# An attention and mixture-of-experts kernel: the attention steps written out as two rows of parts, and smaller routing tables

## The chip, the cores and the metric

The kernel runs on one core of one Trainium2 chip. The metric is the device time of one execution in microseconds (us). A core has five engines that each run their own list of instructions in order and wait for one another by semaphores: TensorE (PE; its weight loads are PEld), VectorE (DVE), ScalarE (ACT), GpSimd (POOL) and SyncE (SP). DMA transfers are issued from the lists of SP, ACT and POOL.

## What is computed

Attention with a linear bias and a window of 128 keys for 8 batches, 8 heads, 576 positions, 64 wide; then, for all 4608 rows, a dense two-layer network plus one of 8 experts, picked by the largest gate logit and weighted by its probability.

```python
scores = scale * q @ k.T;  rel = pos[:, None] - pos[None, :]
scores = where((rel >= 0) & (rel < 128), scores - slope * abs(rel), -1e9)
attn = exp(scores - max);  x = (attn / sum) @ v          # rows of 512: 8 heads x 64
y_dense = maximum(x @ w1_dense, 0) @ w2_dense
e = argmax(x @ w_gate);  gate = softmax(x @ w_gate)[e]
out = y_dense + gate * (maximum(x @ w1[e], 0) @ w2[e])
```

## The kernel before

**Attention.** The work comes in 16 units `u` (a batch and half of its heads, 4 heads), and a unit in three parts `pr`: query tiles 0 and 1, tiles 2 and 3, and the last 64 rows; 48 steps in all. A unit loads q and k (576 KB each, into `qraw` and `kraw`, one buffer each) and v; DVE transposes q and k (`turn`, L157), ACT rounds them (`round_qk`, L166), DVE makes the low half of v (`prep_v`, L176).

A step has this chain: PE writes the bias into `sq` (L371) and adds the scores (L383); ACT takes the exponential (L394, two halves); DVE subtracts the rounded part (`plo`, L413, two halves); PE multiplies by v into `ax` (`attend`, L447); DVE divides (`norm`, L462 and L463) into `xf`, of which there are two buffers; POOL copies `xf` into the row that is sent away (L469), PE transposes it (`flip`, L490) and ACT copies it twice (L497).

**Gate and dense part.** When a batch's six steps are done: logits (L511, L532), choice of expert (L543 to L554), counts on PE (L566, L574), slots (L584 to L601); POOL scatters the rows to `xs_dram` (L609, five transfers), and PE and ACT compute the dense network in 13 pieces (`dense1` L655 with ACT L662, `dense2` L670 with ACT L681), whose results POOL scatters to `ys_dram` (L682, five transfers). All of these pieces pass through two PSUM buffers (`psum_m`). POOL also loads the 18 expert and dense weight blocks (L89).

**Order.** The order on PE, ACT, DVE and SP is as the program issues it; on POOL a scheduler sets it. One loop over 49 passes issues in pass n: the transposes of step n-3, bias and scores and exponentials of step n, the norm of step n-2, `attend` of step n-1, then dense pieces and `turn`, `round_qk` or `prep_v` of the next unit, and last the `plo` of step n:

```python
if 0 <= n - 3 < NS: flip(*steps[n - 3])
if n < NS: lo = scores(u, pr)
if n - 2 in norms: norms.pop(n - 2)()
if 0 <= n - 1 < NS: norms[n - 1] = attend(*steps[n - 1])
... # dense pieces; turn, round_qk, prep_v of unit u + 1
if lo: lo()
```

**Experts.** After 6 batches a table (`route_early`) on one partition gives 16 blocks of 128 rows of one expert; after all 8 a second table (`late_table`) gives 27 more. For each of 43 blocks SP fetches the rows (`fetch`, L871), PE transposes them (L886), DVE brings the expert's first weights (`bring`, L907), PE does both layers (L918, L934), DVE adds (L942) and POOL scatters the result (L950). The leftovers of the last two batches stand between the first blocks.

Of the kernel before, what the change touches and what calls it, by code (L numbers as in the profile page):

```python
# [9 lines left out]
F32 = mybir.dt.float32  # L10
# [13 lines left out]
def kernel(  # L24
# [37 lines left out]
    NL = NB - NE  # L62

# [19 lines left out]
    def load_weights(i):  # L83
        e, wi = divmod(i, 2)
        if e == 0:
            e, src = E, (moe_w1_dense, moe_w2_dense)[wi]
        else:
            e, src = e - 1, (moe_w1, moe_w2)[wi][e - 1]
        nc.gpsimd.dma_start(  # L89
            out=w_all[:, e, wi, :, :],  # L90
            in_=src.rearrange("(ks p) f -> p ks f", p=P),
        )

# [19 lines left out]
    )  # L113

# [102 lines left out]
    last = (NU - 1) % NV  # L217
    order = [i for i in range(NV) if i != last]
    vfs = {i: abuf.tile([P, NT, 4, D + 1], F32, name=f"vf{i}") for i in order}
    for i in range(2):  # L220
        kT = abuf.tile([P, 2, SP_], F32R, name=f"kT{i}")
        nc.gpsimd.memset(kT.bitcast(F32)[:, :, S:SP_], 0.0)
        kTs.append(kT)
    vfs[last] = abuf.tile([P, NT, 4, D + 1], F32, name=f"vf{last}")
    for i in range(NV):
        nc.gpsimd.memset(vfs[i][TAIL:P, NT - 1, :, :], 0.0)
        nc.gpsimd.memset(vfs[i][:, :, :, D : D + 1], 1.0)
    for i in range(2):
        xrow = dbuf.tile([P, NT, RW], F32, name=f"xrow{i}")
        nc.gpsimd.memset(xrow[:, :, TC + 1 : RW], 0.0)  # L230
        xrows.append(xrow)
    lt = dbuf.tile([P, SP_ - DT[1][0] * P], F32, name="ltsb")
    nc.gpsimd.memset(lt, 0.0)
# [33 lines left out]
    def more_constants():  # L267
# [26 lines left out]
        nc.vector.tensor_copy(out=jf, in_=jf_i)  # L294
# [12 lines left out]
    jf = consts.tile([P, NB], F32, name="jf")  # L307
# [5 lines left out]
    def pool_constants():  # L313
# [15 lines left out]
        nc.gpsimd.iota(jf_i, pattern=[[1, NB]], base=0, channel_multiplier=0)  # L329
# [10 lines left out]
    jf_i = ints[:, 128 : 128 + NB]  # L340
    pool_constants()

# [7 lines left out]
    def scores(u, pr):  # L350
        hq = u % HQ
        qT = qkT[("q", u)]
        kT = qkT[("k", u)]
        kjs = KP[pr]
# [3 lines left out]
        wid = PW if len(kjs) == 2 else TAIL  # L358
        tot = wid * len(kjs)

        for rot, g in [(i, j) for i in range(4) for j in range(4)]:
# [16 lines left out]
            )  # L378
        for i, kj in enumerate(kjs):
# [11 lines left out]
        ps = []  # L391
        for i in range(2):
            p32 = ppool.tile([P, 2, tot], F32, name="p32", tag=f"p32_{tot}", bufs=4 if len(kjs) == 2 else 2)
            nc.scalar.activation(  # L394
                out=p32[:, :, 0:tot],
                in_=sq[i][:, :, 0:tot],
                func=ACT.Exp,
                scale=SCALE,
            )
            phi = p32.bitcast(BF16).rearrange("p g (c t) -> p g c t", t=2)[:, :, :, 1]  # L400
            plo = ppool.tile([P, 2, tot], BF16, name="plo", tag=f"plo_{tot}", bufs=4 if len(kjs) == 2 else 2)
            ps.append((p32, phi, plo))
        for i, kj in enumerate(kjs):
            for g in range(4):
                _, phi, plo = ps[g // 2]
                pbuf[(u, kj, g)] = (
                    phi[:, g % 2, i * wid : (i + 1) * wid],
                    plo[:, g % 2, i * wid : (i + 1) * wid],
                )

        def lo():
            for p32, phi, plo in ps:
                nc.vector.tensor_tensor(  # L413
                    out=plo[:, :, 0:tot],
                    in0=p32[:, :, 0:tot],
                    in1=phi[:, :, 0:tot],
                    op=ALU.subtract,
                )

        return lo  # L420
# [3 lines left out]
    def attend(u, pr):  # L424
# [29 lines left out]
        ax_v = ax[:, :, 0 : 4 * (D + 1)].rearrange("p t (h d) -> p t h d", h=4)  # L454

        def norm():
            if hq == 0 and pr == 0:
                cur[("xrow", b)] = xrows[b % 2]
            xrow = cur[("xrow", b)].bitcast(BF16)
            xf = xpool.tile([P, 2, 256], F32, name="xf", tag="xf")  # L460
            recip = gs.tile([P, 2, 4], F32, name="recip", tag="recip")
            nc.vector.reciprocal(out=recip[:rows, 0:nt], in_=ax_v[:rows, 0:nt, :, D])  # L462
            nc.vector.tensor_tensor(  # L463
                out=xf[:rows, 0:nt].rearrange("p t (h d) -> p t h d", h=4),
                in0=ax_v[:rows, 0:nt, :, 0:D],
                in1=recip[:rows, 0:nt].unsqueeze(3).to_broadcast([rows, nt, 4, D]),
                op=ALU.mult,
            )
            nc.gpsimd.tensor_copy(  # L469
                out=xrow[:rows, qis[0] : qis[0] + nt, hq * 256 : hq * 256 + 256],  # L470
                in_=xf[:rows, 0:nt],
            )
            cur[("xf", u, pr)] = cur["xf"] = xf

        return norm

    def flip(u, pr):
# [4 lines left out]
        if hq == 0 and pr == 0:  # L482
            cur[("xTb", b)] = xpool.tile([P, 4, S], BF16, name="xTb", tag="xTb")
        if pr == 0:
            cur["xT"] = xpool.tile([P, 2, S], F32, name="xT", tag="xT", bufs=1)
        xf = cur.pop(("xf", u, pr))
        tp = psum_m.tile([P, 2, 2, P], F32, name="tp", tag="misc")
        for i in range(nt):
# [7 lines left out]
        for dst in (cur["xT"], cur[("xTb", b)][:, 2 * hq : 2 * hq + 2, :]):  # L496
            nc.scalar.copy(  # L497
                out=dst[:, :, q0 : q0 + nt * rows].rearrange(
                    "p c (t x) -> p t c x", t=nt
                ),  # L500
                in_=tp[:, 0:nt, :, 0:rows],
            )
# [3 lines left out]
    def gate_a(u):  # L506
        lp = psum_m.tile([P, 512], F32, name="lp", tag="misc")
        for h, (t0, t1) in enumerate(DT):
            for c in range(2):
# [4 lines left out]
                    rhs=cur["xT"][:, c, t0 * P : t0 * P + LW],  # L514
# [3 lines left out]
        gst["lp"] = lp  # L518

    def gate_av(u):  # L520
        src, dst = gst["lp"][:, 0:LW], lt[:, 0:LW]
# [40 lines left out]
    def gate_c(b):  # L562
# [13 lines left out]
        )  # L576
        ex = gs.tile([P, NT, E], F32, name="ex", tag="ex")
        nc.scalar.activation(out=ex, in_=gst["lgs"], func=ACT.Exp)
        gst["ex"], gst["pc"] = ex, pc
# [12 lines left out]
    def gate_d(b):  # L592
        oh, ex, sl = ohs[b % 2], gst["ex"], gst["sl"]
        xrow = cur[("xrow", b)]
# [7 lines left out]
        nc.gpsimd.tensor_scalar_add(  # L602
# [4 lines left out]
        for t in range(NT):  # L607
            rows = min(P, S - t * P)
            ins = nc.gpsimd.indirect_dma_start(  # L609
                out=xs_dram[:, :],  # L610
                out_offset=bass.IndirectOffsetOnAxis(ap=slot[:rows, t : t + 1], axis=0),
                in_=xrow.bitcast(I32)[:rows, t, :],
                in_offset=None,
            )
            apart("x", b, ins)
        slots[b] = slot

# [26 lines left out]
    def dense1(b, c, hf):  # L644
        c0, c1 = DT[hf][0] * P, min(DT[hf][1] * P, S)
        HF = c1 - c0
        xTb = cur[("xTb", b)]
        if c == 0:
            cur["hT"] = xpool.tile(
# [505 lines left out]
```

## Time and profile before

| | before |
|---|---|
| median of 3 runs (lowest to highest) | 418.57 us (418.14 to 421.89) |
| the profiled execution's own time | 417.28 us |
| its span, first to last instruction | 415.6 us |
| last attention norm ends | 286.8 us |
| busy share of the span PE, DVE, ACT, POOL | 80%, 67%, 66%, 49% |

Shares over the whole span mix the attention stage (up to 287 us) with the expert stage (from there on); the rows below go by stage.

### The profile page before, as it was taken

The numbers are of one execution on the slowest core, as the hardware profiler recorded it, in microseconds if no ns is written. First come the engines' busy times: TensorE is split into PE (matmuls) and PEld (weight loads), VectorE is DVE, ScalarE is ACT, GpSimd is POOL, SyncE is SP. The second block draws the span as 40 slices with busy tenths as digits, with TensorE's granted clock in tenths as the row PEclk, the third lists the DMA queues.
The fourth block names the chain that finished last, engine by engine and source line by source line (L and its number), as shares of the span: only waits on it lengthen the run. The fifth ranks groups of instructions, "written<-read, shape, count | busy, mean of one in ns | idle before, by whom it ended". The sixth has DMA issues, their size and how long they took to land.

```text
span 415.6 us, 12698 instructions
## 1 busy us (share of the span) xinstructions
PE 333.6 (80%) x5003; PEld 228.2 (55%) x5003; DVE 280.3 (67%) x517; ACT 272.7 (66%) x430; POOL 202.0 (49%) x244
## 2 busy tenths in 40 slices
PE   3678887897788789789778976866975889999990
PEld 0455664564455456466555744544743557777770
DVE  5989897966769478686666879553433536666661
ACT  5859777977878597787669785734424445565550
POOL 4023317646444644863643586343173356555562
PEclk9999699999999899999969998997995999999996
DMA  7948799679967595997948816365866849999830
GB/s 204 263 103 166 178 213 216 178 195 217 242 143 182 170 213 169 211 213 184 229 161 171 218 61 125 100 200 165 271 200 216 318 137 311 331 293 334 274 144 14
DMA packets 76731, 82.43 MB, mean 198 GB/s; under 512 B 43519, under 2 KB 61311, under 8 KB 76672
## 3 DMA queue, kind: packets, MB, share of 16 engines
q1 hardware_dynamic: 58704, 47.32, 40.9%
q0 software_dynamic: 17680, 33.12, 30.9%
q10 hardware_dynamic: 288, 1.18, 0.8%
q8 instruction: 40, 0.66, 0.7%
q14 instruction: 19, 0.16, 0.1%
HBM read 64.20 MB, written 28.66 MB: 223 GB/s over the span
## 4 chain that ended last, share of the span: by engine, by line
PE 37%; DVE 19%; issue 12%; POOL 11%; ACT 9%; DMA 7%; another core or an unknown queue 2%; POOLq 1%; DVEq 0%; ACTq 0%; SPq 0%
DVE plo L413 9%; POOL out_dram L950 9%; PE ax L447 9%; PE yp L670 7%; PE hp L655 5%; ACT qT L166 4%; PE sq L383 3%; PE tp L490 3%; DVE xf L463 3%; PE hpm L918 2%; PE lg L532 2%; POOL xs_dram L609 2%; ACT p L394 2%; DVE qs L157 2%; DMA qraw<-in_q_dram 2%
## 5 line engine op out<-in xcount | busy, mean ns | idle before, releaser
L413 DVE TENSOR_TENSOR plo<-p 128x1024 bf16<-128x1024 f32 (+1 forms) x96 | 86.2, 938 | 40.7 <-ACT p L394 38.3
L394 ACT ACTIVATE p<-sq 128x1024 f32<-128x1024 f32 (+1 forms) x96 | 69.8, 784 | 21.2 <-PE ax L447 11.3
L447 PE MATMUL ax<-vf,p 128*128 128x65 bf16 (+1 forms) x576 | 66.7, 204 | 16.2 <-DVE xf L463 14.8
L447 PEld LDWEIGHTS <-p 128*128 128x128 bf16 (+1 forms) x1152 | 62.7, 106 | 30.7 <-DVE xf L463 20.3
L950 POOL DMA_INDIRECT out_dram<-yo,xr x43 | 49.0, 1138 | 52.5 <-DVE yo L942 36.3
L469 POOL CAST xrow<-xf 128x512 bf16<-128x512 f32 (+1 forms) x48 | 39.0, 813 | 69.2 <-DVE xf L463 66.2
L447 PE MATMUL ax<-vl,p 128*128 128x64 bf16 (+1 forms) x576 | 66.2, 200 | 0.7 <-issue 0.7
L447 PE MATMUL ax<-vf,plo 128*128 128x65 bf16 (+1 forms) x576 | 66.0, 201 | 0.9 <-issue 0.9
L942 DVE SCALAR_TENSOR_TENSOR yo<-y,xr,yr 128x512 f32<-128x512 f32 x43 | 32.3, 751 | 47.2 <-issue 17.6
L682 POOL DMA_INDIRECT ys_dram<-yt,slot x35 | 39.9, 1141 | 40.3 <-ACT yt L681 35.0
L447 PEld LDWEIGHTS <-plo 128*128 128x128 bf16 (+1 forms) x576 | 58.4, 105 | 1.1 <-issue 1.1
L655 PE MATMUL hp<-xTb,w_all 128*128 128x256 bf16 (+1 forms) x256 | 44.0, 302 | 7.7 <-ACT hTd L662 3.1
L609 POOL DMA_INDIRECT xs_dram<-xrow,slot x40 | 41.9, 1046 | 12.0 <-issue 10.4
L934 PE MATMUL y<-w_all,hTm 128*128 x172 | 45.8, 389 | 2.3 <-issue 1.2
L918 PE MATMUL hpm<-xTm,ws 128*128 128x128 bf16 x688 | 46.3, 221 | 1.6 <-ACT xTm L892 1.5
L383 PE MATMUL sq<-qT,kT 32*128 32x256 f32 (+2 forms) x640 | 32.5, 313 | 17.9 <-ACT qT L166 10.0
L670 PE MATMUL yp<-w_all,hTd 128*128 128x512 bf16 (+1 forms) x160 | 42.1, 389 | 3.7 <-DVE ltsb L523 1.9
L918 PEld LDWEIGHTS <-ws 128*128 128x128 bf16 x688 | 41.3, 99 | 3.1 <-issue 1.7
L662 ACT ACTIVATE hTd<-hp 128x256 bf16<-128x256 f32 (+1 forms) x64 | 25.8, 422 | 26.1 <-PE hp L655 18.1
L926 ACT ACTIVATE hTm<-hpm 128x512 bf16<-128x512 f32 x43 | 25.7, 598 | 23.0 <-PE hpm L918 11.9
L383 PEld LDWEIGHTS sq<-qT,kT 32*128 32x128 f32 x640 | 24.3, 199 | 27.7 <-ACT qT L166 12.6
L166 ACT CAST kT<-ks 128x1152 fp32r<-128x1152 f32 x16 | 37.8, 2360 | 1.8 <-DVE ks L157 1.8
(138 smaller groups left out, 553.0 us busy)
## 6 DMA issues: line engine op xcount, KB each, us to landing
yr<-ys_dram SPq DMA_DIRECT2D x43, 256.0 KB
kraw<-in_k_dram SPq DMA_DIRECT2D x16, 576.0 KB
vf<-in_v_dram SPq DMA_DIRECT2D x64, 128.0 KB
w_all<-in_moe_w_dram POOLq DMA_DIRECT2D x16, 512.0 KB
qraw<-in_q_dram SPq DMA_DIRECT2D x14, 576.0 KB
xr<-xs_dram SPq DMA_DIRECT2D x43, 130.0 KB
ys_dram<-fill_x SPq DMA_DIRECT2D x8, 256.0 KB
qraw<-in_q_dram ACTq DMA_DIRECT2D x2, 576.0 KB
```

The source lines that it names most:

```text
L166: copy(out=d[:, :, 0:S].rearrange("p c (x r) -> p c r x", r=R), in_=s.rearrange("p c (r x) -> p c r x", r=R),)
L383: nc.tensor.matmul(out=sq[g // 2][:, g % 2, i * wid : i * wid + nq], lhsT=kT[32 * g : 32 * g + 32, c, kj * P : kj * P + P], rhs=qT[32 * g ...
L394: nc.scalar.activation(out=p32[:, :, 0:tot], in_=sq[i][:, :, 0:tot], func=ACT.Exp, scale=SCALE,)
L413: nc.vector.tensor_tensor(out=plo[:, :, 0:tot], in0=p32[:, :, 0:tot], in1=phi[:, :, 0:tot], op=ALU.subtract,)
L447: nc.tensor.matmul(out=ax[:rows, i, o0 : o0 + w], lhsT=lhs, rhs=rhs, start=(n == 1), stop=(n == 3 * len(kl)),)
L609: ins = nc.gpsimd.indirect_dma_start(out=xs_dram[:, :], out_offset=bass.IndirectOffsetOnAxis(ap=slot[:rows, t : t + 1], axis=0), in_=xrow. ...
L655: nc.tensor.matmul(out=hp[:, 0:HF], lhsT=w_all[:, E, 0, kc, c * P : c * P + P], rhs=xTb[:, kc, c0:c1], start=(kc == 0), stop=(kc == 3),)
L670: nc.tensor.matmul(out=yp[:rows, :], lhsT=hT[:, c, t0 * P : t0 * P + rows], rhs=w_all[:, E, 1, c, :], start=(c == 0), stop=(c == 3),)
L682: ins = nc.gpsimd.indirect_dma_start(out=ys_dram[:, :], out_offset=bass.IndirectOffsetOnAxis(ap=slots[b][:rows, t : t + 1], axis=0), in_=y ...
L918: nc.tensor.matmul(out=hp[:, c, :], lhsT=ws[:, kc, c * P : (c + 1) * P], rhs=xT[:, kc, :], start=(kc == 0), stop=(kc == 3),)
L934: nc.tensor.matmul(out=y, lhsT=hT[:, c, :], rhs=w_all[:, bass.DynSlice(er, 1), 1, c, :], start=(c == 0), stop=(c == 3),)
L950: ins = nc.gpsimd.indirect_dma_start(out=out[:, :], out_offset=bass.IndirectOffsetOnAxis(ap=xr.bitcast(I32)[:, TC : TC + 1], axis=0), in_= ...
```

## The change

**Order.** `scores`, `flip` and the others are cut into parts, one for each piece on one engine, and named by a key: `mask` (the bias), `qk`, `exp`, `lo` (one half of `plo`), `ax`, `norm`, `xrow` (POOL's copy), `tp` (transpose), `xT` and `xTb` (ACT's two copies), `tk`, `tq`, `rk`, `rq`, `vl`, `lk`, `lq`, `lv` (loads), `lp`, `lt`, `lg`, `gb`, `pc`, `ex`, `cv`, `gd` (gate), `xs`, `ys` (POOL's scatters), `hp`, `hTd`, `yp`, `yt` (dense), `w` and `wd` (weights). The row `FIRST` (128 parts) orders batch 0. The row `CYCLE` (136 parts) is repeated for batches 1 to 7; a part marked `@1` or `@2` belongs to the batch one or two repetitions back, `@-1` to the next one. The numbers behind a name are half of the heads and step (or piece). POOL's parts of the attention stage are chained in this order too (`in_turn`). Two weight blocks go with each batch (four with batch 0); before, 18 over 42 steps.

**Routing tables.** They stand on 32 partitions, one block on each; the running sums over experts are one product with a triangle and one reduction (`sums`) in place of a copy and seven additions.

**Constants.** `more_constants` is issued before the first `turn`, and its POOL part before the memsets of `vf`, `kT` and `xrow`.

```diff
-        for n in range(NS + 1):
-            if 0 <= n - 3 < NS:
-                flip(*steps[n - 3])
...
+    CYCLE = """
+        xs:1@2 vl:0@0 tp:1,1@1 xTb:1,1@1 tq:1@0 xrow:1,0@1 xT:1,1@1
+        exp:0,0,1@0 lk:1@0 xs:3@2 ax:1,2@1 w:1@1 yp:0@2 yt:0@2 yp:1@2
...
+    for i, word in enumerate(CYCLE):
+        word, late = word.split("@")
+        for b in range(1, B):
+            put(b, word, ((b + int(late)) * L + i, 1, 0))
+    plan = sorted(left, key=left.get)
...
+        for key in plan:
+            at = left[key]
+            if at > end:
+                break
+            n = 6 * at[0] / L
+            do(*key)
...
+    def in_turn(ins):
+        if chain:
+            tc.add_manual_dep(
+                ins.ins,
+                chain[0],
...
+    def sums(cnt, nm):
+        m = rt.tile([RB, E, E], F32, name="m" + nm, tag="m")
+        nc.vector.tensor_tensor(
+            out=m, in0=tri, in1=cnt.unsqueeze(1).to_broadcast([RB, E, E]), op=ALU.mult
+        )
+        cb = small("cb" + nm)
+        nc.vector.tensor_reduce(out=cb, in_=m, op=ALU.add, axis=AX.X)
+        return cb
...
         mask_consts()
+        more_constants()
         turn(0, "k")
```

POOL, from one batch's row scatters on, before (`xs_dram` rows are `xs`, `ys_dram` rows `ys`; the number in a name is a buffer's):

```order
L609 DMA xs_dram<-xrow_144,slot 37888x260 x5
L469 CAST xrow_142<-xf 128x2x256
L701 CAST w_all<-xf 64x1
L89 DMA w_all<-in_moe_w_dram 128x4x512
L602 TENSOR_SCALAR xrow_144<-tok_c 128x5
L682 DMA ys_dram<-yt,slot 37888x512 x2
L469 CAST xrow_142<-xf 64x256
```

And now:

```order
L662 DMA xs_dram<-xrow_168,slot 37888x260
L510 CAST xrow_170<-xf 128x2x256
L662 DMA xs_dram<-xrow_168,slot 37888x260
L768 CAST w_all<-xf 64x1
L91 DMA w_all<-in_moe_w_dram 128x4x512
L510 CAST xrow_170<-xf 128x2x256
L662 DMA xs_dram<-xrow_168,slot 37888x260
L753 DMA ys_dram<-yt,slot 37888x512
L662 DMA xs_dram<-xrow_168,slot 37888x260
L753 DMA ys_dram<-yt,slot 37888x512
L510 CAST xrow_170<-xf 64x256
L662 DMA xs_dram<-xrow_168,slot 37888x260
```

The five scatters in a row are spread among the dense scatters, the copies and a weight load.

DVE in the middle of a batch, before (`ks` and `qs` are the transposed k and q):

```order
L157 STREAM_TRANSPOSE ks<-kraw 128x18x2x32
L413 TENSOR_TENSOR plo<-p_1436 128x1024
L413 TENSOR_TENSOR plo<-p_1439 128x1024
L462 RECIPROCAL recip<-ax 64x4
L463 TENSOR_TENSOR xf<-ax,recip 64x256
L157 STREAM_TRANSPOSE qs<-qraw 128x18x2x32
L413 TENSOR_TENSOR plo<-p_1536 128x1024
L413 TENSOR_TENSOR plo<-p_1539 128x1024
```

And now, behind the transpose of the second unit's k:

```order
L446 TENSOR_TENSOR plo<-p_1555 128x1024
L446 TENSOR_TENSOR plo<-p_1566 128x1024
L496 RECIPROCAL recip<-ax 128x8
L497 TENSOR_TENSOR xf<-ax,recip 128x512
L194 TENSOR_TENSOR vl<-vf_156 128x1280
L572 TENSOR_TENSOR ltsb<-ltsb,lp 128x320
L446 TENSOR_TENSOR plo<-p_1720 128x128
L496 RECIPROCAL recip<-ax 128x8
L497 TENSOR_TENSOR xf<-ax,recip 128x512
L446 TENSOR_TENSOR plo<-p_1664 128x128
L175 STREAM_TRANSPOSE ks<-kraw 128x18x2x32
L175 STREAM_TRANSPOSE qs<-qraw 128x18x2x32
```

Before, a k or a q is transposed in each step; now the next batch's first k and q come one behind the other, ten rows behind the k of the second unit.

SP's loads for a batch, before:

```order
L129 DMA kraw<-in_k_dram 128x1152
L129 DMA qraw<-in_q_dram 128x1152
L149 DMA vf_129<-in_v_dram 128x4x64 x4
L149 DMA vf_129<-in_v_dram 64x4x64
L129 DMA kraw<-in_k_dram 128x1152
```

And now:

```order
L147 DMA kraw<-in_k_dram 128x1152 x2
L147 DMA qraw<-in_q_dram 128x1152
L167 DMA vf_161<-in_v_dram 128x4x64 x4
L167 DMA vf_161<-in_v_dram 64x4x64
L147 DMA qraw<-in_q_dram 128x1152
```

Two loads of k stand in a row; the second waits for the transpose of the first, and the load of q stands behind it.

## Rows read from the trace of the kernel before

**Rows 1.** Windows: three batches (from logits to logits) and the expert stage.

```profile
core 0: us, PE busy (x) PEld busy (x) DVE busy (x) ACT busy (x) POOL busy (x), PEclk, DMA share, GB/s
...
158.60:192.30 33.70, 28.04 (x497) 18.89 (x497) 25.14 (x43) 27.24 (x42) 20.42 (x24) 1.00 0.87 206
192.30:229.20 36.90, 30.61 (x497) 20.54 (x498) 25.49 (x44) 27.31 (x43) 18.46 (x24) 0.91 0.75 183
229.20:266.20 37.00, 29.19 (x497) 19.59 (x497) 30.55 (x78) 27.32 (x42) 21.11 (x22) 0.95 0.52 120
...
287.00:415.60 128.60, 108.08 (x1143) 76.46 (x1141) 66.71 (x124) 60.91 (x112) 62.79 (x58) 0.92 0.72 239
```

**Rows 2.** Chain of waits inside batch 158.6 to 192.3: start, length, what.

```profile
168.80 0.59 PE tp L490 x4
169.39 0.36 PE sq L371 x16
169.75 1.09 issue
170.84 0.74 PE sq L383 x13
171.58 0.97 PE yp L670 x4
...
181.70 2.24 ACT kT L166
...
185.33 2.35 ACT qT L166
```

**Rows 3.** DVE's timeline in the same batch: start, length; in brackets the idle time.

```profile
174.59 2.36 DVE L413 TENSOR_TENSOR plo<-p 128x1024 bf16<-128x1024 f32 x2 [3.46 <-ACT p L394]
```

**Rows 4.** Chain of waits up to 24 us.

```profile
0.80 5.71 DMA kraw<-in_k_dram
...
9.34 6.40 DMA qraw<-in_q_dram
...
19.45 0.14 DVE ut_b L269
...
22.00 0.13 DVE recip L462
```

**Rows 5.** Timelines of DVE and SP: two transposes, a load, batch 0's last norm.

```profile
6.54 1.38 DVE L157 STREAM_TRANSPOSE ks<-kraw 128x1152 f32<-128x1152 f32 x1 [3.08 <-DMA kraw<-in_k_dram]
...
7.95 0.34 SPq L129 DMA_DIRECT2D kraw<-in_k_dram  x1
...
11.96 1.38 DVE L157 STREAM_TRANSPOSE ks<-kraw 128x1152 f32<-128x1152 f32 x1 [0.19 <-DMA kraw<-in_k_dram]
...
43.51 0.42 DVE L463 TENSOR_TENSOR xf<-ax,recip 64x256 f32<-64x256 f32 x1
```

**Rows 6.** Around 256 and 287 us: last weight load on POOL; DVE's rows.

```profile
256.03 0.83 POOL L89 DMA_DIRECT2D w_all<-in_moe_w_dram  x1 [0.31 <-POOL w_all L701]
...
286.43 0.42 DVE L463 TENSOR_TENSOR xf<-ax,recip 64x256 f32<-64x256 f32 x1
287.30 0.69 DVE L907 COPY ws<-w_all 128x2048 bf16 x1 [0.46 <-DVE xf L463]
```

**Rows 7.** POOL's copies and DVE's `plo` by tile: duration ns min/median/max.

```profile
L469 POOL CAST xrow<-xf x48: 392/612/2490, 22.9 to 286.9; 128x512 bf16<-128x512 f32 x32, 64x256 bf16<-64x256 f32 x16
L413 DVE TENSOR_TENSOR plo<-p x96: 250/1216/1630, 13.3 to 274.9; 128x1024 bf16<-128x1024 f32 x64, 128x128 bf16<-128x128 f32 x32
```

**Rows 8.** POOL by line: busy us, mean ns of one; idle before, releaser.

```profile
L609 POOL DMA_INDIRECT xs_dram<-xrow,slot x40 | 41.9, 1046 | 12.0 <-issue 10.4 <-DVE xrow L601 0.8 <-DVE vl L176 0.6
L682 POOL DMA_INDIRECT ys_dram<-yt,slot x35 | 39.9, 1141 | 40.3 <-ACT yt L681 35.0 <-issue 3.0 <-ACT p L394 1.0
L469 POOL CAST xrow<-xf 128x512 bf16<-128x512 f32 (+1 forms) x48 | 39.0, 813 | 69.2 <-DVE xf L463 66.2 <-DVE cbu L762 2.2 <-DVE era L742 0.7
```

**Rows 9.** PE's timeline in the expert stage: one leftover dense piece of 320 columns.

```profile
296.75 0.71 PE L655 MATMUL hp<-xTb,w_all 128*128 128x320 bf16 x4
```

More of the change, by code (lines that the diff above doesn't have):

```diff
@@ L113 @@
     )
+    chain = []
+    def in_turn(ins):
[3 more added lines that the diff above has]
+                chain[0],
+                mybir.DependencyInfo(
+                    mybir.DependencyClass.NoSync, mybir.DependencyReason.DATA
+                ),
+                reason="GpSimd's own order",
+            )
+        chain[:] = [ins.ins.name]
+        return ins
     kTs, xrows = [], []
@@ L215 @@
     )
[L217 to L233, printed above, removed]
     def mask_consts():
@@ L453, in attend, with norm @@
                         )
[L454 to L477, printed above, removed]
+        cur[("ax", u, pr)] = ax
+    def norm(u, pr):
         b, hq = divmod(u, HQ)
@@ new lines @@
+    by_unit = {
+        "lk": load_k,
+        "lq": lambda u: load_q(u, nc.sync),
+        "lv": load_v,
+        "tk": lambda u: turn(u, "k"),
+        "tq": lambda u: turn(u, "q"),
+        "rk": lambda u: round_qk(u, "k"),
+        "rq": lambda u: round_qk(u, "q"),
+        "vl": prep_v,
+        "mask": biases,
+        "qk": scores,
+        "exp": expo,
+        "lo": low,
+        "ax": attend,
+        "norm": norm,
+        "xrow": row_copy,
+        "tp": flip,
+        "xT": lambda u, pr: flip_copy(u, pr, False),
+        "xTb": lambda u, pr: flip_copy(u, pr, True),
+        "lp": gate_a,
+        "lt": gate_av,
+        "w": lambda u: weights(2 + u, ("xf", u, 1)),
+    }
@@ new lines, in table @@
+    def table(cnt, cb, first, nm):
+        wt = wts[0 if first is None else 1]
+        nc.vector.tensor_scalar(
+            out=wt[:, 1, :],
+            in0=cnt[:, 0 : E - 1],
+            scalar1=float(-P),
+            scalar2=float(ST),
+            op0=ALU.mult,
+            op1=ALU.add,
+        )
+        if first is not None:
+            df = small("df" + nm, w=E - 1)
+            nc.vector.tensor_tensor(
+                out=df, in0=first[:, 1:E], in1=first[:, 0 : E - 1], op=ALU.subtract
+            )
+            nc.vector.scalar_tensor_tensor(
+                out=wt[:, 1, :],
+                in0=df,
+                scalar=float(P),
+                in1=wt[:, 1, :],
+                op0=ALU.mult,
+                op1=ALU.add,
+            )
+        ge = small("ge" + nm, w=E - 1)
+        nc.vector.tensor_scalar(
+            out=ge,
+            in0=cb[:, 0 : E - 1],
+            scalar1=pidx_f[0:RB, 0:1],
+            scalar2=None,
+            op0=ALU.is_le,
@@ new lines @@
+        opened, early = False, []
+        end = left[(B - 1, "norm", 1, 2)]
+        for key in plan:
[4 more added lines that the diff above has]
+            do(*key)
+            if key == (NQ - 1, "cv"):
+                gen = route_early()
+                early = [(n + 0.5 + 0.5 * i, lambda g=gen: next(g, None)) for i in range(3)]
+                early.append((n + 2, early_used))
+            while early and n >= early[0][0]:
+                early.pop(0)[1]()
+            if not opened and n >= 6 * B - 3:
+                assert not early
+                if any((B - 1, x, 1) in left for x in ("tk", "rk", "tq", "rq")) or any(
+                    k[0] < NQ for k in left
+                ):
+                    continue
+                opened = True
@@ L1075 @@
                     fetch(j)
-        assert wnext == 2 * (E + 1)
-        norms.pop(NS - 1)()
+        assert opened
+        made = {"hTd": "hp", "yt": "yp", "xT": "tp", "xTb": "tp", "xrow": "norm", "ys": "yt"}
+        for key in plan:
+            if key in left and key[1] in made:
+                if (key[0], made[key[1]]) + key[2:] not in left:
+                    do(*key)
+            elif key in left and key[0] < B - 1 and key[1] in ("gd", "xs"):
+                do(*key)
+        rest = [k for k in plan if k in left and k[0] == B - 2 and k[1] in ("hp", "yp")]
+        assert all(
+            k[1] in ("hp", "hTd", "yp", "yt", "ys") for k in left if k[0] == B - 2
+        ) and all(k[0] >= B - 2 for k in left)
         ph1.close()
@@ L1124 @@
             block(j)
+        assert not left
 _INS = ['q', 'k', 'v', 'moe_w_gate', 'moe_w1_dense', 'moe_w2_dense', 'moe_w1', 'moe_w2']
```

575 lines of the change are left out of this document (320 added, 255 removed).

## The prediction

> **What bounds the kernel now.** First the windows by stage [rows 1]: what is an average there, and which engine leads? From logits to logits a batch takes 33.7 to 37.0 us in the three rows. In it ACT is busy 27.2 to 27.3 us whatever the batch takes, PE 28.0 where its granted clock is 1.00 (2.4 GHz throughout) and 29.2 to 30.6 where it is 0.91 to 0.95, DVE 25.1 to 25.5 (30.6 in the batch with the first routing table), POOL 18.5 to 21.1. So nothing is full: PE stands for some 6 us of each batch, ACT for 7 to 9. The attention stage is bound by waits between engines in a fixed order, not by one engine. Then the chain of waits inside the fastest of these batches, 33.7 us [rows 2]: it goes from PE to ACT's rounding of q (2.35 us) and back to the scores, so while ACT rounds and rereads, PE and DVE run dry: in DVE's timeline 3.46 us of waiting for the exponential in one place [rows 3]. The chain also has pieces named issue, the longest 1.09 us, in which PE waited for nothing that the profile shows. Last the expert stage, 128.6 us, PE busy 108.1 of them [rows 1]: it is near PE's limit and the change touches its edges alone.
>
> **Profile's own time.** The profiled execution took 417.28 us, its span 415.6, so 1.7 lie around the span. The sum below is made on the span; the median of the runs, 418.57, stands 1.3 above the profiled execution.
>
> **The change part by part.**
>
> *Constants.* In the chain up to 24 us the constants stand on DVE from 19.45 to 22.00, on the path to the first norm [rows 4]: 2.55 us. Now they stand ahead of the first transpose. That waits for k, which lands 5.71 us after its issue at 0.80, that is at 6.51 [rows 4]; DVE's idle time just ahead of it is 3.08 us [rows 5], and 2.55 us fit. So −2.6 us; were POOL's constants 3 us late, the cover would be gone and the gain with it. Bounds −2.6 to 0. The load of q behind it (9.34 to 15.74) is on the same path and stays.
>
> *Batch 0.* It ended at 43.9 us (last norm at 43.51, 0.42 long [rows 5]). DVE's rows from the first transpose to that norm come to 29.6 us in the new order (six transposes and the rounding of q, three `vl`, eight large and six small `plo`, six norms), so 6.5 + 29.6 = 36.2 is the floor and 43.9 the ceiling. I take 40.5, nearer the middle: constants −2.6, and 0.8 of the 5 us that remain, since batch 0 still waits for its loads.
>
> *The repeated row.* The floor for a batch is ACT's 27.3 us. To see what waits remain I went through one repetition by hand, part by part, with durations as in the chain (tp 0.59, mask 0.36, qk 0.74, yp 0.97 less overlap, rk 2.24, rq 2.35 [rows 2]) and 0.2 us from an engine's end to the next one's start (a choice above the 0.02 to 0.06 that most hops of the chain show). PE's parts then come to 27.1 us, and PE stands in six places, each 0.1 to 0.4 us: before yp:1 for xT:1,1; before hp:1,2 for hTd:1,0; before ax:0,1 for norm:0,0; before tp:0,1, hp:0,2 and lp:0 for the two PSUM buffers. In all 1.5 us, so 28.6 per batch: parts of two batches lie between producer and consumer, and rk and rq run while PE has attend and dense pieces of an older batch. Three costs come on top. Issue pieces: 1.09 in one place [rows 2]; I take 1.5, bounds 0 to 3, since no row shows what makes them. Loads: the second k of a pair is issued when the k before is transposed, at 7 us of the repetition, and is wanted at 13.2; q right behind at 14.5. Single loads took 5.71, 6.40 and (7.95 to 11.96) 4.0 us with others in flight [rows 4, 5]. So k arrives in time and q 0 to 2 us late; I take 0.5. The granted clock: it cost PE 1.2 and 2.6 us in two of the three batches [rows 1], mostly beside waits; I take 0.4. Sum 31.0 for a batch, bounds 28.6 to 33.7.
>
> *Sum to the end of attention.* Batch 1 has fewer dense parts of older batches: 30 us. Batches 2 to 7: 6 × 31.2 = 187, with half a microsecond for the early table in it (14 short DVE instructions instead of some 30; before, that batch's DVE had 5 us more than others [rows 1]) and nothing to load in batch 7. 40.5 + 30 + 187 = 258, against 286.8 now: −29 us. Bounds by the repetition: 7 × 28.6 + 38 = 238, 7 × 33.7 + 42 = 278.
>
> *The turn to the experts.* `bring` reads w_all at an address known only at run time, so it waits for all 18 blocks. The last was issued at 256.03, 31 us ahead of the first `bring` at 287.30 [rows 6]: free. Now the last (w:1 of batch 7) stands in POOL's row behind norm:1,1, some 4 us ahead of the last norm. A block lands after 4 to 7 us (512 KB against the 576 KB of k and q, which took 4.0 to 6.4 [rows 4, 5]): DVE stands at `bring` 0 to 3.5 us, with all adds behind it, and PE at layer 1 of the first block. I take +2. Against it, batch 6 leaves four dense pieces to the expert stage where seven were left: 3 × 0.7 [rows 9] = −2.1. The late table has 17 short instructions for 31, of 0.15 to 0.2 us; DVE mostly waits for PE there, so −1 of some 2.5. Together −1, bounds −5 to +4.
>
> *POOL.* By the row's means a batch has five `xs` at 1.05 and five `ys` at 1.14 with 0.3 between, six copies at 0.81 and two weight blocks [rows 8]: 22 us of 31, so its fixed order costs nothing while that holds. If it doesn't, see below.
>
> In a row of the profile `plo` takes 1216 ns in the middle and 1630 at most, and POOL's copy 612 and 2490 [rows 7]; 48 copies took 39.0 us, some 13 more than at their medians, so the stretch is mostly POOL's. The Trainium skill ("SBUF — State Buffer", section "Who interferes with whom") says that a DVE instruction with two inputs in SBUF and a GpSimd instruction that reads SBUF cannot run together, and that whichever comes second waits for the whole of the other. That speaks against a denser DVE beside the same copies; the stretched copies agree with it.
>
> **Sum.** 417.28 − 29 − 1 = 387.5 for such an execution, and with the 1.3 that the median stands above it 388.8; I say 388.5. Its own range: repetition 29.6 to 32.6, 378 to 400.
>
> **Rivals.**
> (1) *The pair of loads decides.* For: the loads share the DMA engines, busy 0.75 to 0.87 of these batches [rows 1], and a shorter batch raises that share; k and q are now asked for together with v behind them. Against: the longest single load was 6.4 us. Price: each microsecond that q comes later than 7.3 us after its issue goes into every batch, since `lo`, `gb` and the gate stand behind it on DVE. At 1.5 to 3.5 us: 7 × 2.5 = 17 more, 399 to 413, say 406.
> (2) *DVE is held by POOL's copies.* If the second to come is always DVE, six copies of 0.41 to 0.61 per batch hold it 3.3 us: 7.5 × 3.3 = 25, so 413. Against: `plo` at most 0.41 above its median, and copies that bear the stretch. What decides is which side comes second. The rule of the Trainium skill ("SBUF — State Buffer", section "Who interferes with whom") allows either.
> (3) *Slower: POOL becomes the bound.* POOL's parts are now chained, `xf` has two buffers, and a norm waits for the copy of two norms before; a copy stands behind scatters in the chain. It decides from 31 us of POOL per batch. At the longest rows seen as a rule, `xs` and `ys` 2.1 and copies 1.8, a batch is 22 + 10 + 6 = 38 us: 7 × 7 more, 437. Slower than now begins at 35.4 us a batch. Against: the mean rows above.
> (4) *The order does not take.* In a fixed order one late part holds all behind it, the gaps come back elsewhere, and a batch takes its (286.8 − 43.9) / 7 = 34.7 us again, up to 35.4: what is left is the constants, 413 to 419, say 416.
>
> **How the numbers follow.** This kernel's runs tell about 1% (4 us) from no change. Forecast 378 to 400: 0.62; better than that, the floor of the repetition: 0.08; (1) 0.16; (2) 0.04; (3) 0.05; (4) 0.05. Faster by over 1% (under 414.4): 0.62 + 0.08 + 0.16 + 0.03 and a little of (4), 0.90; within 1% 0.05; slower 0.05. The range reaches down to a repetition of 29 us (374) and up over most of (1): 374 to 410.
>
> **What would show it.** Windows of one batch: 30 to 32 us, ACT's 27.3 at 0.85 or more of it, PE at clock 1.00. DVE's first norm near 20.2, the end of batch 0 near 40.5, the last norm near 258. DVE's transposes wait for DMA under 1 us per batch; if 2 to 4, (1) holds. `plo` with its median near 1216 and copies stretched further: the stretch stays on POOL; a median of 1400 or more: (2). POOL's copies waited for by DVE's norm: (3). The first `bring` waits for w_all 0 to 3.5 us. Wrong would be a batch of 34 us or more, or an expert stage over 133 us.

## The result, and the profile after

The changed kernel took 379.75 us (median of 4 runs, 378.24 to 381.09), the kernel before beside it 418.36 us: ratio 0.912, 95% interval 0.901 to 0.922. The forecast was 388.5, range 374 to 410. The profiled execution took 381.09 us, its span 379.4. Here and below a median is over all runs of a kernel, while a ratio leaves out runs more than 1.5% above that kernel's fastest.

Windows of the changed kernel, from logits to logits as in [rows 1], and the expert stage (same columns):

```profile
88.10:116.30 28.20, 27.21 (x498) 18.83 (x496) 24.17 (x43) 26.83 (x42) 19.44 (x20) 1.00 0.83 218
...
145.10:175.10 30.00, 28.36 (x500) 19.97 (x497) 25.91 (x44) 27.20 (x43) 20.96 (x22) 0.94 0.86 217
...
203.60:234.30 30.70, 27.65 (x500) 18.91 (x496) 25.59 (x57) 26.48 (x43) 22.66 (x20) 1.00 0.65 156
...
250.00:379.40 129.40, 108.11 (x1140) 76.27 (x1138) 64.84 (x115) 60.75 (x111) 69.06 (x65) 0.93 0.77 251
```

A batch takes 28.2 to 30.7 us where it took 33.7 to 37.0, with nearly the same busy time on every engine (the largest difference is DVE's in the batch with the first table, 25.6 against 30.6). ACT is at 0.86 to 0.95 of a batch; what is gone is waiting. From the last norm on the expert stage takes 129.4 us, before 128.8.

DVE's timeline of the changed kernel (start, length; in brackets the idle time ahead and its releaser): batch 0, then the turn to the experts, which answers to [rows 6].

```profile
21.18 0.21 DVE L496 RECIPROCAL recip<-ax 128x8 f32<-128x8 f32 x1 [0.46 <-PE ax L478]
...
25.02 0.21 DVE L496 RECIPROCAL recip<-ax 128x8 f32<-128x8 f32 x1 [2.50 <-PE ax L478]
...
32.17 0.17 DVE L496 RECIPROCAL recip<-ax 64x4 f32<-64x4 f32 x1 [3.68 <-PE ax L478]
...
44.86 0.42 DVE L497 TENSOR_TENSOR xf<-ax,recip 64x256 f32<-64x256 f32 x1
...
249.58 0.42 DVE L497 TENSOR_TENSOR xf<-ax,recip 64x256 f32<-64x256 f32 x1
250.58 1.42 DVE L1089 COPY ws<-w_all 128x2048 bf16 x2 [0.58 <-DVE xf L497]
255.35 1.18 DVE L1089 COPY ws<-w_all 128x2048 bf16 x1 [3.34 <-PE xps L1068]
261.04 0.75 DVE L1124 SCALAR_TENSOR_TENSOR yo<-y,xr,yr 128x512 f32<-128x512 f32 x1 [4.52 <-DMA xr<-xs_dram]
```

Batch 0 ends at 45.28, not earlier than before (43.93): DVE waits 2.5 and 3.7 us for PE. The last norm ends at 250.00, before at 286.85: 36.9 us, the whole gain. The first `bring` starts 0.58 us behind that norm and waits for no weights.

The same kernel's instructions by tile (duration ns min/median/max), which answer to [rows 7]:

```profile
L446 DVE TENSOR_TENSOR plo<-p x96: 268/1183/1450, 14.8 to 246.4; 128x1024 bf16<-128x1024 f32 x64, 128x128 bf16<-128x128 f32 x32
...
L510 POOL CAST xrow<-xf x48: 387/622/6132, 22.3 to 256.0; 128x512 bf16<-128x512 f32 x32, 64x256 bf16<-64x256 f32 x16
...
L175 DVE STREAM_TRANSPOSE ks<-kraw x16: 1359/1366/1380, 6.8 to 222.2; 128x1152 f32<-128x1152 f32 x16
...
  DMA kraw<-in_k_dram: 2.0, 2
```

`plo` did not grow, POOL's copies stretched up to 6.13 us, and DVE's transposes of k waited for their loads twice in all, both times in batch 0 (last line: us, times).

Last, the waits between 104.74 and 250 us, DVE's and PE's (us in total, times, longest):

```profile
DVE xf L497 <- POOL xrow L510: 6.8, 4, 1.8
...
DVE xf L497 <- issue: 3.0, 1, 3.0
...
PE tp L525 <- issue: 0.7, 1, 0.7
```

One new wait: the norm for POOL's copy. The piece of 3.0 us that stands as issue is the same wait: the norm starts at 231.91, and a copy on POOL ends at 231.87. So it is 9.8 us in five places. Of PE's issue pieces one is left in 145 us.

### The profile page after: what moved, and what is told of

Its sections match the earlier page's. It is cut to its first block, busy times and chain, and to the rows that moved or that the text cites. A ratio compares the mean times of both kernels' runs of the same rounds, so it can differ in the third digit from the quotient of the medians.

```text
span 379.4 us, 12661 instructions
## 1 busy us (share of the span) xinstructions
PE 325.6 (86%) x5003; PEld 229.1 (60%) x5003; DVE 273.7 (72%) x487; ACT 271.8 (72%) x430; POOL 223.3 (59%) x247
## 4 chain that ended last, share of the span: by engine, by line
PE 23%; POOL 21%; issue 16%; DVE 16%; DMA 11%; ACT 6%; SPq 2%; another core or an unknown queue 1%; POOLq 1%; DVEq 0%; ACTq 0%
POOL out_dram L1132 11%; PE ax L478 7%; DVE plo L446 6%; DMA ys_dram<-yt,slot 5%; POOL xs_dram L662 4%; PE yp L733 3%; ACT p L435 3%; POOL ys_dram L753 3%; POOL xrow L510 3%; PE hp L706 2%; PE sq L422 2%; DVE xf L497 2%; DMA vf<-in_v_dram 2%; DVE qs L175 2%; PE tp L525 2%
## 5 line engine op out<-in xcount | busy, mean ns | idle before, releaser
L435 ACT ACTIVATE p<-sq 128x1024 f32<-128x1024 f32 (+1 forms) x96 | 74.9, 796 | 14.6 <-PE sq L422 8.9
L662 POOL DMA_INDIRECT xs_dram<-xrow,slot x40 | 48.9, 1223 | 33.4 <-issue 26.1
L478 PE MATMUL ax<-vf,plo 128*128 128x65 bf16 (+1 forms) x576 | 64.6, 200 | 1.0 <-DVE plo L446 0.8
L510 POOL CAST xrow<-xf 128x512 bf16<-128x512 f32 (+1 forms) x48 | 44.7, 933 | 34.7 <-DVE xf L497 27.8
L478 PE MATMUL ax<-vl,p 128*128 128x64 bf16 (+1 forms) x576 | 64.8, 199 | 0.0
L753 POOL DMA_INDIRECT ys_dram<-yt,slot x35 | 45.4, 1298 | 14.7 <-ACT yt L748 6.9
L706 PE MATMUL hp<-xTb,w_all 128*128 128x256 bf16 (+1 forms) x256 | 41.3, 289 | 2.0 <-ACT hTd L721 1.8
L1074 ACT COPY xTm<-xps 128x512 bf16<-128x512 bf16 x43 | 25.2, 585 | 20.0 <-issue 8.2
L497 DVE TENSOR_TENSOR xf<-ax,recip 128x512 f32<-128x512 f32 (+1 forms) x48 | 28.8, 600 | 14.5 <-POOL xrow L510 7.3
L184 ACT CAST qT<-qs 128x1152 fp32r<-128x1152 f32 x15 | 35.8, 2384 | 1.0 <-PE sq L422 1.0
```

Of the source, the lines that this page charges most:

```text
L184: copy(out=d[:, :, 0:S].rearrange("p c (x r) -> p c r x", r=R), in_=s.rearrange("p c (r x) -> p c r x", r=R),)
L435: nc.scalar.activation(out=p32, in_=sqs[(u, pr)][i][:, :, 0:tot], func=ACT.Exp, scale=SCALE)
L478: nc.tensor.matmul(out=ax[:rows, i, o0 : o0 + w], lhsT=lhs, rhs=rhs, start=(n == 1), stop=(n == 3 * len(kl)),)
L510: ins = nc.gpsimd.tensor_copy(out=xrows[b % 2].bitcast(BF16)[:rows, qis[0] : qis[0] + nt, hq * 256 : hq * 256 + 256], in_=cur[("xf", u, pr ...
L662: ins = nc.gpsimd.indirect_dma_start(out=xs_dram[:, :], out_offset=bass.IndirectOffsetOnAxis(ap=slots[b][:rows, t : t + 1], axis=0), in_=x ...
L706: nc.tensor.matmul(out=hp[:, 0 : c1 - c0], lhsT=w_all[:, E, 0, kc, c * P : c * P + P], rhs=cur[("xTb", b)][:, kc, c0:c1], start=(kc == 0), ...
```

## The experiments

They ran in four series, each on one chip with runs of the kernel before beside it. In the first and the third series, on one and the same chip, the kernel before took 383.9 and 383.6 us; in the second and the fourth, on two other chips, 422.6 and 420.4, near the 418.4 of the result (whose chip is not on record). Nothing in my working had room for that. I call the first chip quiet, for the reason that the traces show below. Times are compared within a series, places in traces across them.

**Series 1 (before: 383.93 us).**

*Old order with constants and tables.*

```diff
 (the kernel before, with the new constants' region and table functions)
-                        for i in range(5):
+                        for i in range(3):
...
-            if n == 1:
-                more_constants()
...
+        more_constants()
         turn(0, "k")
```

> The loop of before, with its order, its pacing of weights and POOL left to the scheduler, but with the new tables and the constants ahead of the first transpose. Theory A (the order of the parts on PE, ACT and DVE is the gain): 413 to 418 us, since the first norm moved by only 0.7 us after the change (22.15 to 21.43) and the tables took a few short DVE instructions away. Theory B (constants and tables carry a good part of the 38 us): 405 us or less.

Measured 377.47 us, ratio 0.985 (0.978 to 0.991). So constants and tables are worth some 6 us on this chip, and neither theory meets the rest: here the old order takes no 418 us to begin with, and a gain of 36 us was not there to be shared out. One of its batches, the same columns as above:

```profile
101.70:132.70 31.00, 27.23 (x502) 18.50 (x496) 25.11 (x44) 27.08 (x43) 19.48 (x22) 1.00 0.92 225
```

*Constants back ahead of the first norm.*

```diff
-        more_constants()
         turn(0, "k")
...
+            if key == (0, "norm", 0, 0):
+                more_constants()
             do(*key)
```

> The changed kernel with the constants on DVE back just ahead of the first norm; POOL's part stays early. By the prediction's term they are worth 2.6 us: 382 to 383. By the trace after, in which the first norm came only 0.7 us earlier because PE's products end then, and in which batch 0 later waits for other things: 379.5 to 380.5, no difference to be measured.

Measured 382.68 us (10 runs), ratio to the kernel before 0.997 (0.993 to 1.000). The changed kernel itself was not in this series, so the size of this edit stays open; but the changed order with this one edit is within 1% of the old kernel here.

*The five row scatters of a batch in a row.*

```diff
-        xs:1@2 vl:0@0 tp:1,1@1 xTb:1,1@1 tq:1@0 xrow:1,0@1 xT:1,1@1
+        xs:1@2 xs:3@2 xs:2@2 xs:4@2 xs:0@2 vl:0@0 tp:1,1@1 xTb:1,1@1 tq:1@0
+        xrow:1,0@1 xT:1,1@1
```

(The four other `xs` are taken out of the rows below.)

> The changed kernel with the five row scatters of a batch in one row again, at the head of the repetition; the order on PE, ACT and DVE is that of the changed kernel. Theory A (order of the parts on PE, ACT and DVE): 379 to 384 us, batches of 29 to 29.6 us. Rival C (the gain is that the scatters no longer stand in a row, and with them the pieces named issue on PE went): issue pieces on PE of 1 to 3 us per batch come back, batches of 30.5 to 32 us, 388 to 400 us.

Measured 400.94 us, ratio to the kernel before 1.042 (1.035 to 1.050). The number is about the one that rival C gave (388 to 400), but not by its way: in the attention stage PE has no issue pieces, and on this chip, as the other kernels show, it would not have had them in any case, so rival C wasn't tested here. POOL's row stands behind DVE's slots of that batch, the copies stand behind the row, and DVE's norm behind the copies. Besides, the transposes wait for their loads. DVE's waits, 100 to 260 us:

```profile
DVE xf L497 <- POOL xrow L510: 13.1, 5, 2.6
DVE ks L175 <- DMA kraw<-in_k_dram: 6.2, 4, 1.7
...
DVE qs L175 <- DMA qraw<-in_q_dram: 3.9, 3, 1.4
```

How much of the time each of the two waits made was not separated.

*The last batch's scatters spread over five expert blocks.*

```diff
-            for t in range(NT):
-                do(z, "xs", t)
...
+        for t in range(NT):
+            fill[3 + t].append(lambda t=t: do(z, "xs", t))
```

> The changed kernel with the five row scatters of the last batch spread over five expert blocks in place of five in a row. In the changed kernel PE stands for 6.6 us there (278.7 to 285.3), with ACT and DVE waiting 5.2 and 4.5 us for a releaser that the trace cannot name. If the row of scatters makes that stall: 374 to 377 us. If it belongs to something else there: 379 to 381 us, with the stall still there.

Measured 376.27 us, ratio 0.983 (0.978 to 0.988). Expert stage 122.7 us where the changed kernel had 129.4. But the old order with its five in a row took 122.1 on this chip (253.4 to 375.5), so the chip explains it as well, and the edit is not shown to be what did it.

**Series 2 (before: 422.57 us).**

*The kernel before, unchanged, for its trace.*

> The kernel before, unchanged, to have its profile beside the runs of this series, in which it took 384 us where the first series had 418. If the 34 us are in the attention stage as a whole (batches of 31 us where they were 33.7 to 37): the last attention norm at 255 to 260 us and no long pieces named issue on PE. If they are in the expert stage: the last norm near 287 and that stage 95 us.

Measured 421.6 us: the 418 of the result is this kernel's usual time on this chip as well. Its last norm ends at 292.4, on the quiet chip with its old tables and spread scatters (below) at 260.6. The difference lies in the attention stage. Here is where. PE's, ACT's and POOL's timelines around 140 us:

```profile
139.94 0.19 PE L447 MATMUL ax<-vf,p 128*64 128x65 bf16 x1
140.65 0.21 PE L447 MATMUL ax<-vl,p 128*64 128x64 bf16 x1 [0.52 <-issue]
...
142.07 0.21 PE L447 MATMUL ax<-vf,plo 128*64 128x65 bf16 x1 [1.11 <-issue]
...
142.11 1.02 ACT L394 ACTIVATE p<-sq 128x1024 f32<-128x1024 f32 x1 [3.67 <-PE ax L447]
...
140.05 0.90 POOL L609 DMA_INDIRECT xs_dram<-xrow,slot  x1 [0.31 <-issue]
```

PE stands 0.5 and 1.1 us between two products of one group whose inputs were all there; ACT stands 3.67 us, although the scores it exponentiates were done at 138.3. POOL is at the fourth and fifth of five row scatters. In the old order on the quiet chip the same exponential starts with the scores' end (128.60), in the middle of the same five scatters (125.2 to 131.7):

```profile
128.63 1.94 ACT L409 ACTIVATE p<-sq 128x1024 f32<-128x1024 f32 x2
```

And the windows of the stop (columns as in [rows 1]): with the granted clock at 1.00 PE does nothing for a microsecond, and only behind it the clock falls to its lower level, 0.50, that is 1.2 GHz.

```profile
140.00:141.00 1.00, 0.44 (x5) 0.21 (x4) 0.00 (x0) 0.00 (x0) 0.95 (x2) 1.00 0.91 340
141.00:142.00 1.00, 0.00 (x0) 0.00 (x0) 0.00 (x0) 0.00 (x0) 0.57 (x1) 1.00 0.93 366
142.00:143.00 1.00, 0.93 (x3) 0.39 (x4) 0.00 (x0) 0.89 (x1) 0.00 (x0) 0.60 0.26 93
143.00:144.00 1.00, 1.00 (x3) 0.15 (x1) 0.84 (x1) 1.00 (x3) 0.00 (x0) 0.50 0.01 4
```

So the fall of the clock follows the stop; it doesn't make it.

The trace also has the time at which each signal (the update of a semaphore, for which other engines wait) was recorded. PE's signals for these scores, whose products end at 138.32, are recorded at 142.08 and later, and ACT starts at 142.11: what ACT waited for is a late signal. In this trace the signals of the scores come within 0.03 us of the products' end as a rule, but 1.4 to 3.8 us behind it in seven steps between 70 and 250 us; in the first trace of the same kernel the longest are 3.6 us. The longest stop of this stage stands in the last batch: the products that DVE waits for end at 281.59, PE's next signal is recorded at 286.90, and DVE starts at 286.93. In the three traces of the old order on the quiet chip (series 1 and 3) none of these signals, 96 in each, is more than 0.03 us late.

The traces of the two kinds of chip differ in one more thing. Of the 509 signals that PE's instructions give in the old order, 436 are recorded in either trace of the kernel before with stops, and 502 to 504 on the quiet chip; the changed kernel's traces with stops have 398 and 403 of 477, its relatives on the quiet chip 464 to 469. So the traces with stops lack some 15% of these records. Every run on record has a span and a granted clock, so each was recorded in this way, and a rival stands untested: that the recording itself holds the signals up on some chips, and that an unrecorded execution has no stops. The Trainium skill ("SBUF — State Buffer", section "Who interferes with whom") says that PE and ACT never wait on anyone at SBUF's ports; by that the ports are not the cause, and no run here shows what is.

*The changed kernel, unchanged.*

> The changed kernel, unchanged, beside the kernel before on the same chip. Theory A (the order of the parts takes about 6 us off each batch): 350 to 360 us, if before has 384. Theory D (on this chip the old order has no stalls that the new order could take away, since the old order with constants and tables alone took 377): 377 to 382 us, within 2% of before.

Measured 382.53 us, ratio 0.915 (0.905 to 0.926): the result again, on a chip where the old order has its stops. The last norm ends at 251.3.

*The kernel before with the constants first.*

```diff
+        more_constants()
         turn(0, "k")
...
-            if n == 1:
-                more_constants()
```

> The kernel before with the constants ahead of the first transpose and nothing else. With constants and tables together it took 6.5 us less than before. If the constants make it: 377 to 379 us, and batch 0 ends 2.2 us earlier. If the tables make it: 381 to 384.

Measured 420.79 us, ratio 1.000 (0.994 to 1.007). Batch 0 ends at 42.75 where it ended at 45.75 in the kernel before of this series, so the 3 us are there in the trace; its last norm ends at 288.3, there at 292.4. The times don't show them: the interval is 2.5 us to either side.

*The changed kernel without the chain on POOL.*

```diff
     def in_turn(ins):
-        if chain:
+        if False:
```

> The changed kernel without the chain on POOL, whose order is then the scheduler's (row scatters four or five in a row, right behind two copies). If the fixed place of the scatters on POOL costs or gives nothing: within 3 us of the changed kernel on the same chip. If the chained order costs (a copy stands behind scatters and norms wait for it): 3 to 8 us less. If it is what gains: 390 to 400 us, as with the five scatters in a row in the chain.

Measured 409.55 us, ratio to the kernel before 0.978 (0.969 to 0.988); 27 us more than the changed kernel beside it, and above the 390 to 400 expected if the chain gains. DVE's and POOL's waits, 107 to 250 us:

```profile
DVE xf L497 <- POOL xrow L510: 22.6, 4, 6.9
...
POOL xrow L652 <- issue: 11.7, 2, 5.9
POOL xrow L652 <- DMA xs_dram<-xrow,slot: 10.2, 2, 5.5
```

The scheduler puts the write of a later batch's row numbers into `xrow` (L652) right behind the scatters that read the same buffer. It waits 5 to 6 us for them to land, the copies stand behind it, and DVE's norm behind those, once per batch. This is rival (3) of the prediction with another first piece, and the chain is what keeps it away. The wait is 5.7 us a batch where the changed kernel beside it has 2.0; a batch takes some 35.8 us where that one takes 29.3. So it accounts for 3.6 of some 6.4 us; where the rest comes from is not shown.

**Series 3 (before: 383.55 us).**

*Old order with constants and tables, again.*

> The old order with constants and tables once more. It took 377 us where the kernel before took 384 in the same series, and the kernel before took 418 and 422 in two other series; no kernel of theirs had it beside it. If the tables take 35 us off (by some way that the traces have not shown): 375 to 380 us again whatever the kernel before takes. If what differs is how the chip of a series behaves while POOL issues five scatters in a row: 6 us less than the kernel before in the same series, so 411 to 416 where that takes 418 to 422.

Measured 377.20 us, ratio 0.984 (0.979 to 0.990), as in series 1, on the same chip. The 6 us against the kernel before hold; it has not run on a chip with stops.

*The kernel before with its row scatters spread on POOL.*

```diff
+        in_turn(ins)
...
-        for t in range(NT):
+        send_x(b, range(NT) if b >= NQ else range(1))
...
+                        ends.setdefault(n + 3, []).append(lambda b=b2: send_x(b, (1,)))
+                        gates.setdefault(n + 4, []).append(lambda b=b2: send_x(b, (2,)))
+                        ends.setdefault(n + 4, []).append(lambda b=b2: send_x(b, (3,)))
+                        gates.setdefault(n + 5, []).append(lambda b=b2: send_x(b, (4,)))
```

> The kernel before, with its order on PE, ACT and DVE, old tables and constants; only on POOL the five row scatters of a batch are spread over three passes among copies, dense scatters and weights, in a fixed order. In its trace PE, ACT and DVE stand together for 1 to 4 us at the end of each row of scatters. Rival C (these stops were the gain): 385 to 395 us where the kernel before takes 418 to 422, no such stops but in the expert stage. Theory A (the order on PE, ACT and DVE was the gain): 410 to 422. The fixed order on POOL can itself cost: a copy waits behind a scatter of dense results.

(`in_turn` stands behind each of POOL's parts, so that they keep the order of issue.) Measured 384.19 us, ratio 1.005 (1.001 to 1.008). Where there are no stops, spreading gives nothing. Its batches take 31.0 to 31.6 us. Against it, the old order with constants and tables (same chip) is 2.9 us ahead at the end of batch 0 (41.70 against 44.58; in its second trace 1.6, 42.97) and 7.2 at the last norm (253.4 against 260.6), the rest between the last norms of batches 6 and 7, where the tables stand: constants some 2 to 3, tables some 4 us.

*Spread scatters at the end, and a third buffer for `xf`.*

```diff
-        xf = xpool.tile([P, 2, 256], F32, name="xf", tag="xf")
+        xf = xpool.tile([P, 2, 256], F32, name="xf", tag="xf", bufs=3)
```

> The changed kernel with the last batch's row scatters spread over five expert blocks and three buffers for the normalized rows in place of two. In the changed kernel the norm waited for a copy on POOL 6.8 us in four places. Spread scatters: 4 to 6 us less than the changed kernel; third buffer: up to 1.7 us per batch where DVE has no other slack, 0 to 5 us in all. 372 to 378 us. If the wait for the copy only moves to the next wait: 376 to 378.

Measured 370.45 us, ratio 0.970 (0.962 to 0.979) to the kernel before, and below the 372 to 378 expected; the kernel of series 1 with two buffers took 376.27 on this chip, where the kernel before took 0.4 us more. DVE's waits for the copy (from 104 us to the last norm) with two buffers, and then with three:

```profile
DVE xf L497 <- POOL xrow L510: 11.3, 6, 3.0
```

```profile
DVE xf L497 <- POOL xrow L510: 1.4, 1, 1.4
```

Ten microseconds of waiting went and some 6 came off the time, 4.3 of them by the last norm (251.6 to 247.3). It is the shortest of all kernels here; on a chip with stops it has not run.

**Series 4 (before: 420.43 us).**

*The kernel before with spread row scatters, again.*

> The kernel before with its five row scatters spread on POOL, once more. In a series in which the kernel before took 384 us it took 384 as well. If this series is one in which the kernel before takes 418 to 422: 383 to 392 us by rival C, in which the stops at the end of a row of scatters make the difference between such series and are what the change removed; 412 to 422 by theory A, in which the order on PE, ACT and DVE made the gain. If the kernel before takes 384 here: 384 again, and the question stays where it is.

Measured 414.62 us, ratio 0.990 (0.984 to 0.996). Rival C had 383 to 392, so it falls as I had put it: the row of five is not the condition. But the edit took 1% off here, clear of the interval, and nothing on the quiet chip (1.005), so the spacing seems to have a part in the stops: PE's signals for the scores are over 2 us late in two steps (2.8 us each), in the first trace of the kernel before in three (2.1 to 3.6). PE's stops are there still. The chain of waits from 142 us on:

```profile
142.74 0.26 PE ax L463 x3
143.00 0.51 issue
143.51 0.29 PE ax L463 x4
143.80 0.45 issue
```

POOL's timeline beside it:

```profile
138.47 0.97 POOL L706 DMA_INDIRECT ys_dram<-yt,slot  x1 [0.30 <-ACT yt L705]
139.74 0.97 POOL L706 DMA_INDIRECT ys_dram<-yt,slot  x1 [0.30 <-issue]
141.01 0.97 POOL L631 DMA_INDIRECT xs_dram<-xrow,slot  x1 [0.30 <-issue]
...
142.57 0.91 POOL L631 DMA_INDIRECT xs_dram<-xrow,slot  x1 [0.17 <-issue]
```

Four scatters still stand close, two of them dense ones, so the edit may not have pulled scatters apart far enough, or something else has the larger part. The runs don't decide between these.

## Why the prediction was right

The time is inside the range and the sign and size hold. But the sum was right by terms that were off both ways, and most of the gain came from something that the prediction had no term for (the last part of this section). In that measure it was luck: on the quiet chip, where the kernel before takes 384 us, nearly the same new kernel (series 1, scatters spread at the end) takes 376: a gain of 2%, where the prediction's working has 7%.

**Constants: mechanism right, size right, end wrong.** −2.6 was said; the old order showed −3.0 at the end of batch 0 on a chip with stops and −2.9 and −1.6 on the quiet one. In the changed kernel the first norm came only 0.7 us earlier than before (21.43 against 22.15), since PE's products end at 21.2 (the reciprocal at 21.18 waits for them): I had not looked for what is late next.

**Batch 0: mis-sized.** 40.5 was said, it ended at 45.28. The term counted DVE's rows as if only loads could hold them; DVE waited 6.2 us for PE in two places. From 28 to 36 us PE's granted clock was 0.66 and 0.50:

```profile
28.00:32.00 4.00, 2.95 (x56) 2.47 (x55) 0.50 (x1) 1.71 (x3) 1.06 (x3) 0.66 1.09 152
32.00:36.00 4.00, 1.15 (x29) 0.86 (x27) 3.72 (x5) 4.00 (x6) 3.06 (x1) 0.50 1.09 248
```

**The repeated row: walk right, additions mis-sized.** Batch 1 took 31.0 us (said: 30). The six from 76.24 to 250.00 took 173.8, or 29.0 each, where 31.2 were said: −13. The walk through the row gave 28.6. The 2.4 on top of it are the step that failed: issue pieces were put at 1.5 per batch and one of 0.7 is left; loads at 0.5, and no transpose waited for one from batch 1 on; the clock at 0.4, with two of the last six batches at 0.94. What replaced them is a wait that I had as rival (3), the norm for POOL's copy, 9.8 us in five batches.

**Turn to the experts: −1 was said, +0.6 measured.** The wait of +2 for w_all at `bring` did not come (0.58 us behind the norm); what came late was the rows: DVE waits 4.52 us for `xr`, and its first add starts 11.0 us behind the last norm, before 6.3. And PE, ACT and DVE stop behind the last batch's five scatters, in ACT's and DVE's timelines of the changed kernel:

```profile
284.37 0.60 ACT L1108 ACTIVATE hTm<-hpm 128x512 bf16<-128x512 f32 x1 [5.17 <-remote]
...
284.43 0.75 DVE L1124 SCALAR_TENSOR_TENSOR yo<-y,xr,yr 128x512 f32<-128x512 f32 x1 [4.49 <-remote]
```

The kernel before has a stop there as well, at 308 to 314 (ACT 5.8 us), so it costs little in the comparison.

**Rivals.** (1), loads: fell in this run (its share of 0.75 to 0.87 left out the third of [rows 1], 0.52); on the quiet chip, with the scatters in a row, it is part of what was seen. (2), DVE held by POOL: fell; `plo`'s median went from 1216 to 1183 ns, and the stretch stayed on POOL's copies. The rule of the Trainium skill ("SBUF — State Buffer", section "Who interferes with whom"), that the second to come waits, agrees: the copy of 6.13 us starts at 32.94, behind DVE's `vl` at 32.80. It lasts until DVE has done not that one instruction but `vl` and four `plo` (38.81). (3), POOL as bound: real at 2.0 us per batch, and at 5.7 without the chain. (4), the order does not take: wrong here.

**What the order gives where there are no stops.** There the old order takes 31.0 us a batch, not 34.7, and with constants and tables ends attention at 253.4 (and 253.2 again), the new one at 251.6. If that carries over, then of the 36.9 us some 7 are constants and tables, 2 the order's own, and the rest is that the new order stopped little where the old one did. My reason for the gain, longer distances between producer and consumer, is therefore shown for a small part alone. I had read the waits of [rows 2, 3] as the order's own; of the 3.46 us in [rows 3] some 1.9 are a late signal (in that trace the scores end at 171.58, PE's signal comes at 173.51). Here are the waits of the old order between 100 and 240 us (total, times, longest), with stops (series 2, PE and DVE):

```profile
PE sq L383 <- ACT qT L166: 6.7, 6, 1.1
PE ax L447 <- issue: 4.8, 8, 1.1
...
DVE plo L413 <- ACT p L394: 27.9, 11, 5.3
```

and on the quiet chip (series 1):

```profile
PE sq L398 <- ACT qT L168: 10.0, 9, 1.1
...
DVE plo L428 <- ACT p L409: 14.5, 9, 2.6
```

The pieces of 1.1 us ahead of the scores are on both chips: that is PE's wait for q's rounding, which [rows 2] call issue and which I had booked as unknown. The pieces inside `ax` are the stops, and with them DVE's wait for the exponential is twice as long. Shown: the stops and the late signals (old order, on the chips of series 2 and 4), their absence (same order, quiet chip), and that in the new order's attention stage little is left of them (the two longest in either trace: near 69 us ACT starts 1.7 us behind its input, near 232 PE's signals for the scores are 2.0 us late). Not shown: what makes them, whether they are there without recording, and which feature of the new order avoids them. POOL's fixed order must stay (27 us without it, over half of it by a wait of its own).

## What to carry to other kernels

Before a wait is put down to the order of instructions, look whether the engine that waits had its inputs: a pause between two products of one group, or an engine idle behind a finished producer, may be no wait of the program, and the same kernel may not have it on another chip: here the signal, and not the product, was late. Time the kernel before on more than one chip when a gain is this much larger than what the removed instructions cost. A term for a fixed order on a side engine (POOL here) is worth an experiment of its own: one buffer more took 6 us off, one manual chain less added 27.

## What the runs showed that I had not expected

- One program, two times: the kernel before took 418.4 to 422.6 us in three series and 383.6 to 383.9 in two, both on one chip. The changed kernel took 379.8 and 382.5; on the quiet chip it has only near relatives, 376.3 and 382.7.
- PE, ACT and DVE stop together, for 0.5 to 4 us and once for 5, with inputs ready while POOL issues scatters close together. PE's signals are recorded up to 5.3 us behind its products; PE's granted clock is 1.00 in the stop shown and 0.50 behind it.
- A copy on POOL that takes 0.39 us alone took 6.13 while DVE worked on `vl` and `plo` without a pause.
